# ConvNeXt-V2 block: smaller rstd batches, reordered GpSimd work, and one more slot between read and use

## Chip, cores, metric

The kernel runs on one core of a Trainium2 chip. The metric is device time in microseconds (us), the median of several executions.

## The reference, cut to what matters

```python
# x: 1 x 512 x 512 x 96 bf16; dw: 3x3 depthwise; w1: 96 -> 384; w2: 384 -> 96
out = depthwise_conv3x3(x, dw)
h = layernorm(out, axis=-1, eps=1e-5)
h = gelu_tanh(h @ w1)
gx = sqrt((h * h).sum(axis=(1, 2)) + 1e-6)          # over the whole image
nx = gx / (gx.mean(axis=-1) + 1e-6)
h = grn_gamma * (h * nx) + grn_beta + h
return x + h @ w2
```

The sum over the whole image cuts the kernel into two phases. Phase one computes convolution, layer norm, first matmul and GELU for all pixels and gathers statistics. Phase two, which needs these statistics, does the second matmul and writes the output. The change touches phase one only.

The layer norm divides by a standard deviation. Its reciprocal, called rstd, is computed for a batch of blocks at a time: six small operations on VectorE (DVE) give the variance and a first guess of the root, which Newton's iteration on GpSimd (POOL in the profiles) refines. PE and ACT are TensorE and ScalarE. `y_bf` is the convolution's output, `yn` the normalised block, `ynT` the same in the layout that the first matmul reads, and `gt` or `g` the output of GELU.

## The kernel before: the parts that matter

Phase one works in slots. A slot does the convolution of one block of 4 image rows (128 blocks) and, for an earlier block, each later stage. How many slots lie between the stages is set by constants, and each engine runs its own work in program order.

```python
NEWTON_ITERS = 3
LAG_ST, LAG_NORM, LAG_MLP = 2, 5, 3
# batches of blocks that share one rstd computation: 2, 2, 4, then 8 each
...
# conv_chunks(b), the end of a slot
act.activation(out=y[:], in_=Y[:], func=ACTF.Identity)              # y_bf <- Y, PSUM eviction
pool.tensor_tensor(out=q[:], in0=y[:], in1=y[:], op=ALU.mult)       # square: ysq <- y_bf
...
# stage_chain(k): six small DVE operations, mean, nmsq, var, clamp+eps, shift, seed of the root
# stage_newton(k): on GpSimd, 4 small operations in each Newton round
# stage_turn(k): DVE transpose rt <- rstd;  stage_rows(k): SP writes r_dram <- rt (4 DMAs)
# stage_bcast(k): SP reads rbc <- r_dram (4 DMAs)
# stage_norm(b):  GpSimd, yn <- y_bf * rbc
# stage_write(b): SP, yn_dram <- yn;   stage_read(b): SP, ynT <- yn_dram (changes the layout)
# mlp_units(b): per j: 4 matmuls U <- ynT,w1p, 2 GELUs gt <- U on ACT, 4 bn_stats on DVE;
#               for 3 blocks of 8 (RECOMP_PATTERN) SP also writes g_dram <- gt, 3 x 512 KB
...
put(last_s, ("chain", k))            # last_s: the slot of the batch's last statistics
put(last_s + 1, ("rows", k))
put(last_s + 3, ("bcast", k))
for b in batch:
    s = max(last_norm + 1, last_s + LAG_NORM)
    put(s, ("norm", b)); put(s + 1, ("write", b)); put(s + 2, ("read", b))
    put(s + LAG_MLP, ("mlp", b))
...
# the order of one slot in the program
write; load_x piece (transposing DMA xT <- x); read; bcast; load_x piece
norm
matmuls of MLP and convolution, interleaved; evac (with the square)
chain; newton; combine; turn; rows
```

A yn block is read in slot s+2 and used in slot s+3. All DMAs of the steady state are issued by SP (SyncE), one after the other; where one has to wait, the ones behind it wait too. In phase two, blocks of g that were stored are loaded, and the others are recomputed from yn.

## Time and profile before

| | before |
|---|---|
| median of 2 runs | 1887.39 us (1886.64 to 1888.15) |
| profiled span | 1883.5 us |
| phase one, to the end of the last bn_stats | 1296.2 us |
| the rest, phase two | 587.4 us |
| 8 slots, mean from the 32nd to the 112th y_bf eviction | (1022.7 - 271.0) / 10 = 75.2 us per 8 slots |

"32nd" counts from 0: the times at which ACT starts its y_bf evictions mark the slots.

The profile page of before: the span, the busy time of each engine, then DVE's busy share and PE's granted clock in 40 equal slices, in tenths.

```profile
span 1883.5 us, 58748 instructions
PE 1454.8 (77%) x25398; PEld 705.7 (37%) x25642; DVE 1443.5 (77%) x2340; ACT 1383.2 (73%) x1381; POOL 965.5 (51%) x733
...
DVE  2354586878878778778787788897788888888887
...
PEclk9887797888888878888888788696999999999999
```

No engine is full: DVE is mostly at 7 to 8 tenths in phase one (the first 27 slices), and PE's granted clock is mostly at 7 to 8 tenths where phase two has 9.

The table of windows of before, cut at the starts of eight successive y_bf evictions. Columns: busy us of each engine (number of instructions), granted clock, DMA share, GB/s. The share is the sum of packet times over 16 engines, so it can be above 1 where packets overlap. `...` stands for lines left out.

```profile
core 0: us, PE busy (x) PEld busy (x) DVE busy (x) ACT busy (x) POOL busy (x), PEclk, DMA share, GB/s
647.10:654.40 7.30, 6.69 (x144) 2.54 (x147) 7.17 (x13) 7.14 (x8) 5.82 (x3) 1.00 1.32 214
654.40:661.70 7.30, 5.25 (x117) 1.50 (x117) 7.13 (x17) 7.14 (x9) 4.73 (x7) 1.00 0.88 296
661.70:677.00 15.30, 11.25 (x168) 3.52 (x171) 9.95 (x18) 7.38 (x9) 13.33 (x14) 0.55 0.74 140
...
691.50:706.60 15.10, 9.45 (x144) 2.81 (x147) 8.23 (x14) 7.41 (x8) 5.86 (x3) 0.66 1.19 252
706.60:713.90 7.30, 6.32 (x142) 2.45 (x144) 6.45 (x11) 7.13 (x9) 5.77 (x2) 1.00 0.37 144
```

Six slots of eight take 7.3 us, in which ACT is full and DVE nearly so. Two take 15 us, with the clock down to 0.55 and 0.66; in and after them DMA runs partly empty (140 and 144 GB/s). The timelines show how a long slot begins. PE first, then SP for the time before it (start us, us, what, idle time before it and what ended it):

```profile
660.66 0.42 PE L37 MATMUL Y<-xT,Wd 32*32 32x511 bf16 x12
665.04 1.46 PE L37 MATMUL U<-ynT,w1p 128*128 128x512 bf16 x3 [3.95 <-DMA ynT<-yn_dram]
```

```profile
651.21 3.65 SPq L37 DMA_DIRECT2D g_dram<-gt  x3
654.96 0.55 SPq L37 DMA_DIRECT2D yn_dram<-yn  x1
655.60 1.59 SPq L37 DMA_TRANSPOSE xT<-in_x_dram  x1
657.25 0.57 SPq L37 DMA_DIRECT2D ynT<-yn_dram  x1
```

The read is issued at 657.25, behind three g writes, a yn write and a transpose. PE waits for it from 661.1, just before the next slot begins, and gets it at 665.0. The waits of before, first of engines, then of SP's own queue, from 300 to 1000 us (total us, times, longest):

```profile
DVE bst L37 <- ACT gt L37: 142.4, 73, 7.1
PE U L37 <- DMA ynT<-yn_dram: 125.6, 44, 7.6
```

```profile
SPq L37 <- ACT gt L37: 106.5, 54, 7.4
SPq L37 <- POOL yn L37: 50.7, 27, 2.4
SPq L37 <- DVE rt L37: 46.6, 9, 6.2
```

Besides g (`ACT gt`), SP waits for the normalise (`POOL yn`) before each write and, once per batch, for the transposed rstd (`DVE rt`) before the rows.

### The profile page before, as it was taken

How to read it: one execution, taken by the hardware profiler on the slowest of the kernel's cores; microseconds unless marked ns; L12 is line 12 of the kernel's file. 1: busy time of each engine (PE TensorE's matmuls, PEld its weight loads, DVE VectorE, ACT ScalarE, POOL GpSimd, SP SyncE). 2: the span in 40 equal slices, each digit the busy share in tenths (PEclk: the TensorE clock that was granted, in tenths of full speed). 3: DMA queues.
4: the chain of work that ended last, by engine and by line, in shares of the span. 5: the costliest groups of instructions: out<-in, count | busy, mean ns of one | idle time of the engine just before them, and what ended most of it. 6: DMA issues, size and time to landing. Idle time of an engine off the chain costs nothing.

```text
span 1883.5 us, 58748 instructions
## 1 busy us (share of the span) xinstructions
PE 1454.8 (77%) x25398; PEld 705.7 (37%) x25642; DVE 1443.5 (77%) x2340; ACT 1383.2 (73%) x1381; POOL 965.5 (51%) x733
## 2 busy tenths in 40 slices
PE   6778676777777777768777677462999999999998
PEld 3323222222222222222222222111666666666666
DVE  2354586878878778778787788897788888888887
ACT  2455586877878768778787688593887887887887
POOL 6765766768668667686686676621121121121120
PEclk9887797888888878888888788696999999999999
DMA  9996999899999998998999986564999999999996
GB/s 121 191 212 129 194 244 219 198 234 219 212 226 205 240 224 198 228 218 210 233 207 243 212 199 214 150 226 153 365 356 375 372 362 374 371 360 373 370 362 231
DMA packets 473012, 472.21 MB, mean 251 GB/s; under 512 B 298576, under 2 KB 394928, under 8 KB 472752
## 3 DMA queue, kind: packets, MB, share of 16 engines
q1 hardware_dynamic: 420144, 348.88, 73.0%
q0 software_dynamic: 20608, 88.09, 12.8%
q10 hardware_dynamic: 32000, 31.46, 5.5%
q8 instruction: 200, 3.28, 0.7%
q14 instruction: 60, 0.49, 0.1%
HBM read 224.55 MB, written 176.69 MB: 213 GB/s over the span
## 4 chain that ended last, share of the span: by engine, by line
PE 34%; ACT 18%; DMA 17%; DVE 5%; issue 4%; SPq 3%; another core or an unknown queue 2%; POOL 0%; ACTq 0%; DVEq 0%
DMA ynT<-yn_dram 16%; ACT gl L203 15%; PE U L37 10%; PE O L587 10%; PE Y L37 8%; DVE bst L37 5%; PE U L201 4%; SPq L37 3%; ACT y_bf L37 2%; PE S L37 2%; ACT gt L37 1%; DMA xr<-in_x_dram 0%; DMA out_dram<-o_sb 0%; DVE o_sb L589 0%
## 5 line engine op out<-in xcount | busy, mean ns | idle before, releaser
L37 DVE BATCH_NORM_STATS2 bst<-gt 128x6 f32<-128x512 bf16 x1536 | 928.3, 678 | 264.8 <-ACT gt L37 261.7
L37 ACT ACTIVATE gt<-U 128x1024 bf16<-128x1024 f32 x768 | 755.1, 1033 | 291.4 <-issue 185.1
L37 PE MATMUL U<-ynT,w1p 128*128 128x512 bf16 x1309 | 463.5, 436 | 267.9 <-DMA ynT<-yn_dram 213.2
L203 ACT ACTIVATE gl<-U 128x1024 bf16<-128x1024 f32 x480 | 457.6, 1028 | 106.2 <-PE U L201 98.1
L37 POOL TENSOR_TENSOR ysq<-y_bf 128x1536 bf16<-128x1536 bf16 x128 | 351.3, 2746 | 321.0 <-ACT y_bf L37 319.1
L37 PE MATMUL Y<-xT,Wd 32*32 32x512 bf16 x13806 | 414.9, 423 | 71.0 <-issue 21.3
L37 POOL TENSOR_TENSOR yn<-y_bf,rbc 128x1536 bf16<-128x1536 bf16 x128 | 395.0, 3089 | 6.7 <-DMA rbc<-r_dram 4.2
L587 PE MATMUL O<-W2s,gl 128*128 128x96 bf16 x6096 | 350.4, 206 | 19.7 <-ACT gl L203 5.1
L587 PEld LDWEIGHTS <-gl 128*128 128x128 bf16 x6096 | 304.2, 97 | 140.4 <-ACT gl L203 54.0
L37 PEld LDWEIGHTS <-w1p 128*128 128x128 bf16 x1536 | 115.1, 102 | 606.6 <-issue 343.0
L589 DVE TENSOR_TENSOR o_sb<-O,xb 128x384 bf16<-128x384 f32 x512 | 257.2, 551 | 100.0 <-PE O L587 90.1
L201 PE MATMUL U<-ynl,w1p 96*128 96x512 bf16 x960 | 283.4, 379 | 51.6 <-ACT gl L203 28.2
L187 POOL DMA_DIRECT2D xr<-in_x_dram x127 | 68.6, 540 | 433.8 <-DVE xb L578 376.6
L37 ACT ACTIVATE y_bf<-Y 128x1536 bf16<-128x1536 f32 x128 | 185.1, 1446 | 61.6 <-PE Y L37 61.6
L578 DVE TENSOR_TENSOR xb<-xr,B2bc_f 128x1536 f32<-128x1536 bf16 x127 | 222.8, 1755 | 9.1 <-DMA xr<-in_x_dram 6.3
L37 PEld LDWEIGHTS <-Wd 32*32 32x32 bf16 x13806 | 118.4, 89 | 272.5 <-issue 263.7
L201 PEld LDWEIGHTS <-w1p 96*128 96x128 bf16 x960 | 76.6, 98 | 88.5 <-issue 72.7
L37 PEld LDWEIGHTS <-y_bf 128*128 128x128 bf16 x1536 | 59.9, 101 | 36.1 <-issue 17.1
L37 PE MATMUL S<-rowsel,y_bf 128*128 128x4 bf16 x1536 | 59.1, 168 | 0.0
L37 PE MATMUL S<-rowsel,ysq 128*128 128x4 bf16 x1536 | 57.4, 167 | 0.0
L37 PEld LDWEIGHTS <-ysq 128*128 128x128 bf16 x1536 | 48.6, 99 | 0.0
L181 POOL DMA_DIRECT2D gl<-g_dram x71 | 37.6, 533 | 7.0 <-DVE W2s L552 3.9
(67 smaller groups left out, 224.9 us busy)
## 6 DMA issues: line engine op xcount, KB each, us to landing
g_dram<-gt SPq DMA_DIRECT2D x144, 512.0 KB, 5.9
yn_dram<-yn SPq DMA_DIRECT2D x128, 384.0 KB, 3.7
ynT<-yn_dram SPq DMA_DIRECT2D x128, 384.0 KB, 4.8
out_dram<-o_sb SPq DMA_DIRECT2D x128, 384.0 KB, 7.7
xr<-in_x_dram POOLq DMA_DIRECT2D x127, 384.0 KB, 7.4
gl<-g_dram POOLq DMA_DIRECT2D x71, 512.0 KB, 10.0
gl<-g_dram SPq DMA_DIRECT2D x70, 512.0 KB, 10.3
ynl<-yn_dram ACTq DMA_DIRECT2D x80, 384.0 KB, 11.5
```

The lines of the kernel that those rows point to most:

```text
L37: r = f(*a, **k)
L181: ld_engs[ldi[0] % 2].dma_start(out=gts[j][:], in_=g_dram[q, j])
L187: nc.gpsimd.dma_start(out=xr[:], in_=x[0, r0:r0 + GR].rearrange("r w c -> (r w) c").rearrange("(p g) c -> p g c", g=PXP))
L201: nc.tensor.matmul(U[:, i, :], lhsT=w1p[:C, j * 128:(j + 1) * 128], rhs=ynt[:, i0 + i, :], start=True, stop=True)
L203: nc.scalar.activation(out=perm_view(gts[j][:, :], i0, 2), in_=perm_src(U[:]), func=ACTF.Gelu_apprx_tanh)
L578: nc.vector.tensor_tensor(out=xb[:], in0=xr[:], in1=B2bc_f[:, None, :].to_broadcast([128, PXP, C]), op=ALU.add)
L587: nc.tensor.matmul(O[:, gl_, :], lhsT=gts[j][:, gg * 128:(gg + 1) * 128], rhs=W2s[:, j, :], start=(j == 0), stop=(j == NCH - 1))
L589: nc.vector.tensor_tensor(out=o_sb[:, sub * GPS:(sub + 1) * GPS, :], in0=O[:], in1=xb[:, sub * GPS:(sub + 1) * GPS, :], op=ALU.add)
```

## The change

Its intent: give GpSimd's normalise and square the right of way over Newton, let nothing on SP wait for the rstd, and leave the yn read another slot to land.

```diff
-NEWTON_ITERS = 3
+NEWTON_ITERS = 2
+BATCH = 4
-LAG_MLP = 3
+LAG_MLP = 4
@@ batches_of: 2, 2, 4, 8, 8, ... becomes 2, 2, 4, 4, ...; tiles and buffer counts follow
@@ the square leaves the eviction and is a stage of its own, a slot later
+        for b in range(NBLK):
+            put(b + 1, ("square", b))
             put(last_s, ("chain", k))
-            put(last_s + 1, ("rows", k))
+            put(last_s + 1, ("newton", k))
+            put(last_s + 1, ("turn", k))
+            put(last_s + 2, ("rows", k))
@@ the order of one slot
             for f in pieces:
                 f()
+            for k in get("rows"):
+                stage_rows(k)
             for b in get("norm"):
                 stage_norm(b)
+            for b in get("square"):
+                stage_square(b)
+            for k in get("newton"):
+                stage_newton(k)
+            for k in get("combine"):
+                combine(k)
@@ ... matmuls ...
+            for k in get("chain"):
+                stage_chain(k)
             if evac:
                 evac()
-            for k in get("chain"):
-                stage_chain(k)
-            for k in get("chain"):
-                stage_newton(k)
-            for k in get("combine"):
-                combine(k)
-            for k in get("rows"):
+            for k in get("turn"):
                 stage_turn(k)
-                stage_rows(k)
```

More of the change, by code (lines that the diff above doesn't have):

```diff
@@ L46, in batches_of @@
     out, b = [], 0
-    for n in (2, 2, 4):
-        if b + n <= nblk:
+    for n in (2, 2) + (BATCH,) * nblk:
+        n = min(n, nblk - b)
+        if n:
             out.append((b, n))
             b += n
-    while b < nblk:
-        n = min(8, nblk - b)
-        out.append((b, n))
-        b += n
     return out
@@ L84 @@
     NBLK = H // GR
+    NB = BATCH * GR * NG
     BATCHES = batches_of(NBLK)
@@ L213 @@
         xtpool = p1.enter_context(tc.tile_pool(name="xt", bufs=X_AHEAD + 3))
-        ypool = p1.enter_context(tc.tile_pool(name="ybf", bufs=8 + LAG_ST + LAG_NORM + 1))
+        ypool = p1.enter_context(tc.tile_pool(name="ybf", bufs=BATCH + 1 + LAG_ST + LAG_NORM + 1))
         ysqpool = p1.enter_context(tc.tile_pool(name="ysq", bufs=4))
         small = p1.enter_context(tc.tile_pool(name="small", bufs=2))
-        rtpool = p1.enter_context(tc.tile_pool(name="rt", bufs=2))
-        rbcpool = p1.enter_context(tc.tile_pool(name="rbc", bufs=3))
+        rtpool = p1.enter_context(tc.tile_pool(name="rt", bufs=3))
+        rbcpool = p1.enter_context(tc.tile_pool(name="rbc", bufs=4))
         ynpool = p1.enter_context(tc.tile_pool(name="yn", bufs=3))
@@ L288, in evac, with stage_square @@
                 ybf[b] = y
-                q = ysqpool.tile([128, NI, W], bf16, name="ysq")
-                pool.tensor_tensor(out=q[:], in0=y[:], in1=y[:], op=ALU.mult)
-                ysq[b] = q
             return [lambda n=n: tap(n) for n in range(9)], evac
+        def stage_square(b):
+            q = ysqpool.tile([128, NI, W], bf16, name="ysq")
+            pool.tensor_tensor(out=q[:], in0=ybf[b][:], in1=ybf[b][:], op=ALU.mult)
+            ysq[b] = q
         def stage_stats(b):
@@ L298, in stage_stats @@
             if b == b0:
-                Ss[k] = psS.tile([128, 2, 128], f32, name="S")
+                Ss[k] = psS.tile([128, 2, NB], f32, name="S")
             S = Ss[k]
@@ L313, in stage_chain @@
             S = Ss.pop(k)
-            mean = small.tile([128, 128], f32, name="mean")
+            mean = small.tile([128, NB], f32, name="mean")
             dve.tensor_scalar(out=mean[:, :N], in0=S[:, 0, :N], scalar1=1.0 / C, scalar2=None, op0=ALU.mult)
-            nmsq = small.tile([128, 128], f32, name="nmsq")
+            nmsq = small.tile([128, NB], f32, name="nmsq")
             dve.scalar_tensor_tensor(out=nmsq[:, :N], in0=S[:, 0, :N], scalar=-1.0 / C, in1=mean[:, :N],
                                      op0=ALU.mult, op1=ALU.mult)
-            var = small.tile([128, 128], f32, name="var")
+            var = small.tile([128, NB], f32, name="var")
             dve.scalar_tensor_tensor(out=var[:, :N], in0=S[:, 1, :N], scalar=1.0 / C, in1=nmsq[:, :N],
@@ L322, in stage_chain @@
             dve.tensor_scalar(out=var[:, :N], in0=var[:, :N], scalar1=0.0, scalar2=LN_EPS, op0=ALU.max, op1=ALU.add)
-            ri = small.tile([128, 128], i32, name="ri")
+            ri = small.tile([128, NB], i32, name="ri")
             dve.tensor_scalar(out=ri[:, :N], in0=var[:, :N].bitcast(i32), scalar1=1, scalar2=None,
@@ L336, in stage_newton @@
                 last = it == NEWTON_ITERS - 1
-                t_ = small.tile([128, 128], f32, name="nt")
+                t_ = small.tile([128, NB], f32, name="nt")
                 pool.tensor_tensor(out=t_[:, :N], in0=rcur, in1=rcur, op=ALU.mult)
@@ L340, in stage_newton @@
                 pool.tensor_scalar(out=t_[:, :N], in0=t_[:, :N], scalar1=-0.5, scalar2=1.5, op0=ALU.mult, op1=ALU.add)
-                rn = small.tile([128, 128], bf16 if last else f32, name="rstd" if last else "rn")
+                rn = small.tile([128, NB], bf16 if last else f32, name="rstd" if last else "rn")
                 pool.tensor_tensor(out=rn[:, :N], in0=rcur, in1=t_[:, :N], op=ALU.mult)
@@ L348, in stage_turn @@
             N = n * GR * NG
-            rt = rtpool.tile([128, 128], bf16, name="rt")
+            rt = rtpool.tile([128, NB], bf16, name="rt")
             dve.transpose(out=rt[:, :N], in_=rstds.pop(k)[:, :N])
@@ L365, in stage_bcast @@
             b0, n = BATCHES[k]
-            rbc = rbcpool.tile([128, 8, W], bf16, name="rbc")
+            rbc = rbcpool.tile([128, BATCH, W], bf16, name="rbc")
             for j in range(GR):
@@ L439 @@
         last_stat_slot = -1
+        for b in range(NBLK):
+            put(b + 1, ("square", b))
         for k, (b0, n) in enumerate(BATCHES):
             for b in range(b0, b0 + n):
-                s = b + LAG_ST
+                last_s = b + LAG_ST
                 if b == b0:
-                    s = max(s, last_stat_slot + 2)
-                put(max(s, b + LAG_ST), ("stats", b))
-                last_s = max(s, b + LAG_ST)
+                    last_s = max(last_s, last_stat_slot + 2)
+                put(last_s, ("stats", b))
             last_stat_slot = last_s
             put(last_s, ("chain", k))
-            put(last_s + 1, ("rows", k))
+            put(last_s + 1, ("newton", k))
+            put(last_s + 1, ("turn", k))
+            put(last_s + 2, ("rows", k))
             put(last_s + 3, ("bcast", k))
@@ L485 @@
             taps, evac = conv_chunks(s) if s < NBLK else ([], None)
-            for b in get("stats"):
-                pass
             stats = [lambda b=b: stage_stats(b) for b in get("stats")]
```

## The prediction

> **What bounds it now.** The table of windows puts phase two (1300 to 1883 us) at 355 GB/s and DMA share 1.00; the diff does not touch it. Phase one ends at about 1297 us (last bn_stats) and is not pinned to one engine: per 150 us between 300 and 1050, DVE is busy 119, ACT 115, PE 109 to 114, GpSimd 105. The starts of the y_bf evictions show why: per 8 blocks, six slots take 7.3 us and two about 15, 75 us in all. The 7.3 us slot is ACT's (1.45 + 6 x 1.03 us, slightly overlapped) and nearly DVE's (12 bn_stats, 7.21 us). In the long slots PE waits 4 to 6 us for ynT<-yn_dram (waits view: 129 us of these 750; 16% of the chain), then runs at a granted clock of 0.50 to 0.53 for about a slot. The Trainium skill, "TensorE: Matmul & The Clock Gate" (Part 1), has an idle PE at half clock; this trace agrees.
>
> The read is issued only a slot before use and lands in 4.1 to 9.3 us. Ahead of it in SyncE's order stand three 512 KB g_dram writes, transposes that back up (issue 1.2 to 5.2 us), or, once per batch, the rstd rows (SP waits 53 us in ten batches for rt) while GpSimd's Newton (5.6 us) and combine (1.7 us) delay the next normalise.
>
> **What the change does.** LAG_MLP 4 gives the read one more slot, 7.3 us or more: above the observed waits. Newton follows normalise and square and delays neither; normalise can run ahead. Newton: 12 operations of 0.30 to 0.45 us become 8 of 0.24 to 0.32, about 6 us per 8 blocks either way. Cost: DVE's chain and transpose run twice per 8 blocks, about 1.6 us each against 1.9 once: DVE needs 58 + 3.3 = 61.3 us per 8 blocks and becomes the engine floor. GpSimd needs 54.5. rbc and r_dram move the same bytes in twice the DMAs. Slots without MLP in between fall from six to two, the last MLP from slot 144 to 141.
>
> **Second limit: DMA.** Its share is 0.94, but some 16% of the time is nearly idle. I estimate DMA's demand at 58 to 63 us per 8 blocks, level with DVE, so I expect 65 to 67 us, not 58.
>
> **Sum.** Steady state: 12.5 groups of 8 x (75 - 66) = 113 us; ramp-up about 30; drain about 30. Total about 172 us, nearly all critical: the phases are serial.
>
> Predicted: 1715 us, range 1665 to 1790; faster by over 2%: 0.94, within 2%: 0.04, slower: 0.02.
>
> **Right if:** slots become even at 7.8 to 8.5 us; PE's wait for ynT falls from 213 us to under 60; phase one's granted clock rises from 0.85 towards 0.95; DVE is busy over 90% from 300 to 1050 us; GB/s there rises from 219 to about 250; phase two stays at 583 us.
>
> **Wrong if:** the transposes really need about 2 us of DMA each, as they took alone in the first 40 us (18 in 36): then DMA holds the slot near 8.8 us and the gain is about 80 us. The skill's "DMA: Bandwidth & Descriptors" (Issuing engines are not separate DMA queues) has all queues share 16 DMA engines; slack adds no bandwidth. Or if lagging DVE delays chain and transpose, and SP, waiting for rt, holds back g writes and reads, so that ynT waits return.

## The result, and the profile after

The changed kernel takes 1705.33 us (median of 2, 1702.93 to 1707.72), a ratio of 0.9035 with a 95% interval of 0.8979 to 0.9092.

| | before | after |
|---|---|---|
| start to 32nd eviction | 271.0 | 247.3 |
| 32nd to 112th eviction | 751.7 | 646.5 (64.6 per 8 slots) |
| 112th to last (127th) eviction | 138.5 | 115.8 |
| last eviction to end of last bn_stats | 135.0 | 109.8 |
| phase two | 587.4 | 581.7 |
| PE's wait for ynT, whole run | 213.2 | 66.0 |

Phase one gives 177 of the 182 us: 128 in the 95 slots after the 32nd, 24 at the start, 25 in the drain, where MLPs run with no convolution beside them. The same lines of the page as before:

```profile
span 1701.1 us, 59162 instructions
PE 1399.3 (82%) x25377; PEld 693.7 (41%) x25624; DVE 1476.4 (87%) x2445; ACT 1381.1 (81%) x1381; POOL 959.8 (56%) x781
...
DVE  2169999999999999999999999978888888888887
...
PEclk9899989989998999989999998869999999999999
```

DVE is now at nine tenths in nearly every slice of phase one, and phase one's granted clock at 8 or 9 tenths. The table of windows after, again cut at evictions (four of the eight slots that were looked at; the other four take 7.3 to 7.4 us), and below it how its long slot begins on PE:

```profile
core 0: us, PE busy (x) PEld busy (x) DVE busy (x) ACT busy (x) POOL busy (x), PEclk, DMA share, GB/s
642.90:650.20 7.30, 5.75 (x118) 1.71 (x120) 7.16 (x12) 7.14 (x8) 5.09 (x2) 1.00 1.41 228
650.20:657.50 7.30, 6.25 (x164) 2.67 (x165) 7.27 (x13) 7.13 (x8) 6.37 (x11) 1.00 0.98 293
657.50:670.20 12.70, 9.10 (x144) 2.59 (x147) 12.70 (x23) 7.40 (x8) 11.25 (x4) 0.73 1.14 253
670.20:677.50 7.30, 6.32 (x142) 2.46 (x144) 6.55 (x12) 7.13 (x9) 5.77 (x2) 1.00 1.10 314
```

```profile
660.33 1.04 PE L38 MATMUL U<-ynT,w1p 128*128 128x512 bf16 x4 [3.40 <-DMA ynT<-yn_dram]
```

One long slot is left in these eight. It too begins with PE waiting for ynT (3.40 us) and has a lowered clock (0.73). It differs from the first long one of before in two columns: DVE is busy for all of its 12.70 us, working off a backlog (23 operations in it, while ACT makes GELUs for about half as many), and DMA is not empty in it (253 GB/s). The waits after, from 300 to 1000 us, engines and then SP:

```profile
PE U L38 <- DMA ynT<-yn_dram: 44.0, 24, 5.5
DVE bst L38 <- ACT gt L38: 21.3, 25, 2.5
```

```profile
SPq L38 <- PE U L38: 99.7, 76, 3.7
SPq L38 <- PE Y L38: 24.1, 21, 2.5
SPq L38 <- ACT gt L38: 24.0, 39, 1.5
```

SP's waits for yn and rt have left the head of the list. It waits for PE to free buffers, so it runs ahead. PE still waits 44 us for ynT, but DVE only 21 us for GELUs, where it waited 142. The windows of the steady state say what has filled up instead, before and then after:

```profile
300.00:1000.00 700.00, 518.86 (x10560) 182.73 (x10706) 554.42 (x956) 535.92 (x521) 492.30 (x285) 0.86 0.95 221
```

```profile
300.00:1000.00 700.00, 575.80 (x12393) 207.80 (x12556) 674.45 (x1193) 625.67 (x612) 568.65 (x373) 0.94 1.15 255
```

DVE rises from 79% to 96% of the time, and DMA share from 0.95 to 1.15. Counted from the packet records in steps of 0.25 us over the same 700 us, DMA was less than half full in 15.3% of the steps before and in 0.8% after. So two resources look full after the change, and the profile alone doesn't say which one holds the time. It also doesn't say which part of the change did the work. The experiments ask both.

One more thing is new. DVE's timeline and GpSimd's, after:

```profile
647.05 0.23 DVE L38 SCALAR_TENSOR_TENSOR var<-S,nmsq 128x64 f32<-128x64 f32 x1
647.31 0.94 DVE L38 TENSOR_SCALAR var<-var 128x64 f32<-128x64 f32 x1
648.28 2.67 DVE L38 TENSOR_SCALAR ri<-var 128x64 int32<-128x64 int32 x1
```

```profile
645.11 3.09 POOL L38 TENSOR_TENSOR yn<-y_bf,rbc 128x1536 bf16<-128x1536 bf16 x1 [5.06 <-DMA rbc<-r_dram]
648.16 2.75 POOL L38 TENSOR_TENSOR ysq<-y_bf 128x1536 bf16<-128x1536 bf16 x1
```

Two tiny operations take 0.94 and 2.67 us, and each ends (648.25, 650.95) about 50 ns after a GpSimd operation ends (648.20, 650.91). Of the 99 such DVE operations 27 took over 0.4 us, and all 27 ended 37 to 56 ns after the end of a GpSimd operation; before it was 6 of 54. The Trainium skill, "SBUF — State Buffer" (Who interferes with whom), describes this: DVE and GpSimd share a port pair as an exclusive lock, which a `tensor_scalar` between SBUF tiles can need; the trace agrees. The operations that read PSUM (`var<-S,nmsq` and its like) stayed at 0.19 to 0.23 us. In the old order GpSimd had mostly just finished its square and waited for the chain. In the new order it is often in a square or a normalise. From 300 to 1000 us one batch's chain with its transpose sums to 2.7 us of DVE, where the prediction had 1.6.

### The profile page after: what moved, and what is told of

It is laid out like the page before. It is cut to its first block, busy times and chain, and to the rows that moved or that the text cites. A ratio compares the mean times of both kernels' runs of the same rounds, so it can differ in the third digit from the quotient of the medians.

```text
span 1701.1 us, 59162 instructions
## 1 busy us (share of the span) xinstructions
PE 1399.3 (82%) x25377; PEld 693.7 (41%) x25624; DVE 1476.4 (87%) x2445; ACT 1381.1 (81%) x1381; POOL 959.8 (56%) x781
## 5 line engine op out<-in xcount | busy, mean ns | idle before, releaser
L38 PE MATMUL U<-ynT,w1p 128*128 128x512 bf16 x1303 | 433.9, 407 | 134.2 <-ACT gt L38 66.8
L38 PE MATMUL Y<-xT,Wd 32*32 32x512 bf16 x13806 | 394.4, 401 | 72.9 <-ACT y_bf L38 28.2
L38 PEld LDWEIGHTS <-w1p 128*128 128x128 bf16 x1536 | 110.7, 99 | 444.0 <-issue 339.5
L38 PEld LDWEIGHTS <-y_bf 128*128 128x128 bf16 x1536 | 56.2, 97 | 26.2 <-issue 5.9
L38 DVE TENSOR_SCALAR mean<-S 128x64 f32<-128x64 f32 (+1 forms) x33 | 6.8, 207 | 49.3 <-PE S L38 49.3
```

Source lines behind the costliest of these rows:

```text
L38: r = f(*a, **k)
```

## The experiments

"Per 8" is the time from the 32nd to the 112th eviction over 10, and "phase one" the end of the last bn_stats, both of the profiled run. Each experiment ran in 3 rounds (e1 to e4, e5 to e8 and e9 to e12 together); the kernel before had medians of 1885.63 to 1888.21 us beside them. The kernel after ran in rounds of its own, so that it meets the experiments only by its ratio. All outputs are right.

| run | median us | ratio (95%) | per 8 | phase one |
|---|---|---|---|---|
| before | 1887.39 | | 75.2 | 1296 |
| after | 1705.33 | 0.9035 (0.8979 to 0.9092) | 64.6 | 1119 |
| e1 before, LAG_MLP 4 | 1725.09 | 0.9154 (0.9123 to 0.9186) | 64.4 | 1132 |
| e2 after, LAG_MLP 3 | 1760.80 | 0.9360 (0.9318 to 0.9402) | 68.4 | 1174 |
| e3 after, batches of 8 | 1710.39 | 0.9080 (0.9050 to 0.9109) | 63.8 | 1126 |
| e4 after, chain's tail on GpSimd | 1703.49 | 0.9033 (0.9003 to 0.9063) | 64.4 | 1118 |
| e5 after, 2 of 8 stored | 1722.81 | 0.9127 (0.9113 to 0.9140) | 60.7 | 1068 |
| e6 e4 and e5 together | 1718.87 | 0.9110 (0.9096 to 0.9123) | 60.4 | 1063 |
| e7 before, new order only | 1771.29 | 0.9402 (0.9372 to 0.9431) | 67.6 | 1178 |
| e8 before, batches of 4 only | 1890.49 | 1.0025 (1.0006 to 1.0044) | 76.9 | 1299 |
| e9 after, old order | 1695.43 | 0.8994 (0.8962 to 0.9025) | 64.4 | 1112 |
| e10 after, 3 Newton rounds | 1700.67 | 0.9029 (0.8979 to 0.9079) | 64.0 | 1115 |
| e11 after, stores moved to the drain | 1673.05 | 0.8866 (0.8825 to 0.8907) | 61.9 | 1080 |
| e12 e11 and e4 together | 1671.80 | 0.8862 (0.8823 to 0.8901) | 62.4 | 1092 |

### e1: the slack alone

```diff
 # on before
-LAG_MLP = 3
+LAG_MLP = 4
```

> The kernel before with LAG_MLP 4 alone (batches of 8, three Newton rounds, old order). Theory A, late yn reads: the one slot of slack between read and use is most of the gain; about 1745 us (1715 to 1780), PE's wait for ynT from 300 to 1050 us falls from 129 us to under 50. Rival B, GpSimd order and batch size: slack alone gives little; 1840 us or more, ynT waits over 90 us.

Measured: 1725 us, inside theory A's range. One constant gives 161 us of the 182, and the steady state is that of the full change (64.4 per 8). The wait for ynT is down from 125.6 us:

```profile
PE U L37 <- DMA ynT<-yn_dram: 33.5, 23, 3.2
```

What the full change has over it, some 20 us, lies outside the steady state, and is a difference of two effects. e1 needs 136 us from its last eviction to its last bn_stats (995.5 to 1132.0), where the changed kernel needs 110, as its last MLP comes in slot 145, not in slot 141, and its phase two is 6 us longer (587.5 us). But it reaches its 32nd eviction 15 us earlier (232.4 us, where the changed kernel has 247.3).

### e2: the change without the slack

```diff
 # on after
-LAG_MLP = 4
+LAG_MLP = 3
```

> The changed kernel with LAG_MLP back at 3. Theory A, late yn reads: most of the gain is lost, about 1830 us (1790 to 1870), two long slots per 8 come back. Rival B, GpSimd order and batch size: it stays near 1740 us or below.

Measured: 1761 us, below the range of theory A and above that of theory B: both missed. Without slack the rest of the change still gains 126 us. So the two halves of the change are substitutes for the most part: 161 and 126 do not add up to 182.

### e7 and e8: which part of the rest

e7 is before with the new order on GpSimd and SP (square, Newton, turn and rows as in the change), with batches of 8, LAG_MLP 3 and three Newton rounds; rbc has 3 and rt 2 buffers as before, y_bf one more than before (17). e8 is before with batches of 4 only:

```diff
 # e8, on before
-        n = min(8, nblk - b)
+        n = min(4, nblk - b)
```

> Old slack and batches of 8, three Newton rounds; only the new order is kept (square a slot later after normalise, Newton after both, rstd rows a slot later). The changed kernel with LAG_MLP 3 gained 126 us; this and the next run say from which part. Theory A2, order: normalise runs ahead, so writes and reads leave earlier: 1740 to 1800 us. Rival B2, batches of 4: 1850 to 1890.

> The kernel before with batches of 4 alone. Theory A2, order: Newton now delays normalise twice per 8 blocks and SP waits for rt twice, so 1860 to 1920 us, apart from some 20 us won at the start by fewer bubbles. Rival B2, batches of 4: 1780 or less.

Measured: 1771 us and 1890 us, both inside the ranges of theory A2. The order alone gains 117 us; smaller batches alone gain nothing. The side remark on e8, some 20 us won at the start, was wrong: its 32nd eviction comes at 286.1 us, 15 later than in before, and only its drain is shorter (107.9 instead of 135.0 us). SP's waits, 300 to 1000 us, show the mechanism. First e7, then e8:

```profile
SPq L38 <- ACT gt L38: 158.9, 88, 5.9
...
SPq L38 <- DVE rt L38: 8.8, 9, 1.6
SPq L38 <- POOL nt L38: 5.1, 8, 1.3
SPq L38 <- POOL rn L38: 1.1, 1, 1.1
```

```profile
SPq L37 <- DVE rt L37: 133.8, 19, 10.4
```

A wait is put down to the GpSimd operation that came last, so yn's waits in e7 are the POOL lines together (a third one, of 0.2 us, is left out). With the new order they are 6 us where before had over 50, and those for rt are 8.8 instead of 46.6: in e7 the median normalise is over 5.8 us before its write is issued, in before 0.5 us. SP's waits fall less as a whole, from 305 to 251 us: it now comes early at the g writes (158.9 us, where before had 106.5). PE's wait for ynT in the same 700 us falls from 125.6 to 64.0 us, so the order cures about half of it. With twice as many batches in the old order, the wait for rt grows to 133.8 us, and everything behind it in SP's order waits too. In the changed kernel the new order takes this cost away, or the slack hides it (e9).

### e9: the slack and the batches of 4, old order

```diff
 # on after: square in the slot of its eviction, Newton in the slot of its chain, both after evac
-            put(b + 1, ("square", b))
+            put(b, ("square", b))
-            put(last_s + 1, ("newton", k))
+            put(last_s, ("newton", k))
```

> The changed kernel (batches of 4, LAG_MLP 4, two Newton rounds) with the old order on GpSimd: square right after the eviction, Newton right after the chain and ahead of the next normalise. If the slack alone brings phase one to DMA's limit (the other lag-4 kernels all ran about 64.5 us per 8 blocks), the order is worth nothing on top: 1695 to 1725 us. If Newton ahead of normalise still costs with batches of 4 (alone they gained nothing): 1740 or more.

Measured: 1695 us, if anything faster than the changed kernel, though the intervals overlap. Once the read has its extra slot, the order of GpSimd's work is worth nothing with batches of 4. The rows are still issued a slot later here, so this run doesn't try that part of the change by itself.

### e3 and e10: batch size and Newton rounds on top of the rest

e3 is the changed kernel with batches 2, 2, 4, 8, 8, ... (one rbc and one rt buffer fewer, so that it fits). e10 has `NEWTON_ITERS = 3`.

> The changed kernel with batches of 8 again (2, 2, 4, then 8; one rbc and one rt buffer fewer so that it fits). Theory A, late yn reads: batch size is not what matters, 1685 to 1735 us: DVE saves one chain per 8 blocks (about 2.7 us measured with its waits), some 30 us lost again to bubbles at the start and a longer drain. Rival B, batch size: 1780 us or more.

> The changed kernel with three Newton rounds: 1.4 us more on GpSimd per batch of 4, about 57 of 64.5 us per 8 blocks. Theory: GpSimd is not the limit, 1697 to 1715 us. If it is: 1720 or more.

Measured: 1710 and 1701 us, both as the theory said and neither distinct from the changed kernel. Of the 30 us that batches of 8 were expected to lose at both ends, e3 lost 10: its drain is 26 us longer (135.4 us), but its 32nd eviction comes 15 us earlier (231.8 us). e3 is also e1 with the new order, the later rows, two Newton rounds and one more y_bf buffer, and in the same rounds it is 15 us faster, with intervals that don't meet. So with batches of 8 these together are still worth a little beside the slack; which of them, no run says. GpSimd, at 81% of the steady state after the change (568.65 of 700 us), is not its limit.

### e4, e5, e6: what limits phase one now

e4 takes the port waits away from DVE:

```diff
 # on after, stage_chain loses its last three operations; stage_newton begins with
+            pool.tensor_scalar(out=var[:, :N], in0=var[:, :N], scalar1=0.0, scalar2=LN_EPS, op0=ALU.max, op1=ALU.add)
+            pool.tensor_scalar(out=ri[:, :N], in0=var[:, :N].bitcast(i32), scalar1=-0.5, scalar2=float(0x5F3759DF),
+                               op0=ALU.mult, op1=ALU.add)
```

e5 takes g writes away from phase one; e6 is both.

```diff
 # e5, on after
-    RECOMP_PATTERN = [False, True, True, False, True, True, False, True]
+    RECOMP_PATTERN = [False, True, True, True, False, True, True, True]
```

> The changed kernel with the last three operations of DVE's chain, the fp32 and int32 SBUF to SBUF tensor_scalar ones, done as two operations on GpSimd. In the profile after, 21 of these from 150 us on took 0.5 to 2.7 us instead of 0.2, each ending about 50 ns after a GpSimd operation. Theory C, DVE is the limit now and loses about 1.0 us per batch to the wait for GpSimd's port: DVE needs 59.7 instead of 63.3 us per 8 blocks, total falls by 35 to 55 us to about 1660. Rival D, DMA is the limit now (share 1.11, nearly never idle): total stays within 12 us of 1705.

> The changed kernel with 2 of 8 blocks of g stored instead of 3 (the recompute pattern), so that phase one writes about 1.6 MB of 16 MB less per 8 blocks; the result stays right, phase two recomputes 16 blocks more. Theory D, DMA is phase one's limit after the change: phase one's end falls from 1118 us, but only to DVE's own 63.3 us per 8 blocks (chain with its port waits): to 1095 to 1108. Rival C, DVE alone is the limit: stays within 5 us of 1118. Phase two 585 to 610 us either way; the total is not the test.

> The same with the chain's last three operations on GpSimd as well. If DMA and DVE are near-equal limits after the change (each removed alone shows little), removing both shows: phase one's end falls to 1060 to 1085 us, about 61 us per 8 blocks, total 1650 to 1685. If neither is the limit: end of phase one over 1100.

Measured, e4: 1703 us, so theory D. DVE's busy time in the 700 us fell from 674 to 643 us and the slots did not move. The port waits cost DVE time that it had. e1 and e9 say the same: they run at 64.4 us per 8 with DVE busy for 647 and 657 us. Measured, e5: phase one ends at 1068, even below theory D's range. The windows of e5 from 300 to 1000 us:

```profile
300.00:1000.00 700.00, 614.18 (x12714) 215.99 (x12713) 692.77 (x1272) 660.82 (x651) 599.08 (x401) 0.97 1.12 241
```

With a tenth of the traffic gone, slots go from 64.6 to 60.7 us per 8, DVE is at 99%, and PE's wait for ynT is 5 us. So the DMA path was the limit of the changed kernel, through reads that came late (PE waited 44 us for ynT there), and DVE is the next. DMA's share is still 1.12 in e5: a high share by itself does not say that DMA is the limit. 96 bn_stats of 0.60 us and two chains of 1.7 us are 61 us per 8 blocks. My range for e5 was off because I had counted DVE's floor with the port waits (2.7 us per chain). In e5 they mostly don't occur: 11 of 99 operations took over 0.4 us, and the chain is back at 1.7 us. Why they vanish there was not tried. They are as few with the old order (e9: 10 of 99, 1.6 us per chain) and with the new order and batches of 8 (e3: 5 of 54), so the new order does not bring them by itself. e6 gains only 5 us more in phase one; by then ACT, at 7.3 us per slot or 58.2 per 8, is near (60.4 measured), but that it is the limit there was not shown. The totals of e5 and e6 are worse than the changed kernel's, because phase two grew from 582 to 654 us; I had expected 585 to 610, and so a total for e6 that it missed.

### e11 and e12: using it

In the drain, after the last convolution, DMA is not full: from 1010 to 1070 us of the changed kernel its share is 0.67. So e11 stores as many blocks of g as before (48), but the last 14 all belong to them, and only 34 of the first 114. Phase two takes the blocks in an order that keeps its mix of loaded and recomputed ones.

```diff
 # on after
-    def is_recomp(q):
-        return RECOMP_PATTERN[q % len(RECOMP_PATTERN)]
+    TAIL, EARLY = 14, 34
+    HEAD = NBLK - TAIL
+    stored = [b for b in range(HEAD) if b * EARLY // HEAD != (b - 1) * EARLY // HEAD] + list(range(HEAD, NBLK))
+    redone = [b for b in range(NBLK) if b not in stored]
+    s_, r_ = iter(stored), iter(redone)
+    ORDER = [next(s_) if i % 8 in (0, 3, 6) else next(r_) for i in range(NBLK)]
+
+    def is_recomp(q):
+        return q not in stored
 # and phase two walks through ORDER instead of range(NBLK)
```

> The changed kernel with the same 48 stored blocks of g, but 14 of them the last 14 (in the drain, where DMA is at half load) and 34 spread over the other 114; phase two takes the blocks in an order that keeps its old mix. DMA as phase one's limit says 2.4 instead of 3 stored blocks per 8 take about 62 us: phase one ends at 1085 to 1100, phase two stays at 583 to 595, total 1675 to 1695. If DMA is not the limit: 1700 or more.

> The same with the chain's last three operations on GpSimd, so that DVE needs about 59.5 instead of 61 to 63 us per 8 blocks: phase one ends at 1070 to 1095, total 1660 to 1690, at most 15 us below the run before.

Measured: 1673 and 1672 us, 11% better than before in the same rounds; against the changed kernel, which ran in other rounds, the medians are 2% lower. e9 and e10, which equal the changed kernel within the noise, ran in e11's rounds and took 1695 and 1701 us. e11 did slightly better than its ranges: phase one ends at 1080 us (1085 to 1100 expected). In e11 the steady state takes 61.9 us per 8, and phase two stays at 582 us. Adding e4's edit is again worth nothing that can be told from noise: single runs of either kernel spread from 1664 to 1679 us.

## Why the prediction was right

- **Total.** 1715 us was predicted, 1705 measured. The terms: steady state 113 against 128 us measured, start 30 against 24, drain 30 against 25, and 6 us that were not predicted between the phases and in phase two.
- **Start and drain, in part luck.** The only reasons that the prediction names for these two terms come from the smaller batches: fewer slots without MLP and an earlier last one. Batches of 4 alone (e8) gain 12 us in the two together, as they lose 15 at the start; the slack alone (e1) gains 37, all of it at the start. The sum of 49 us comes mainly from the slack.
- **Cause.** Late ynT reads: right. Slack alone (e1) brings the steady state to where the full change has it. The half clock came and went with these waits (0.86 before, 0.94 in e1); no run changed it alone. The prediction names the new order too, but did not see that it is a second cure for the same wait, which gives 117 us by itself (e7): once normalise runs ahead, writes and reads leave SP earlier. With the slack and batches of 4 in place it brings nothing (e9).
- **"Slots become even at 7.8 to 8.5 us":** right in the mean (8.1), wrong in form. Most slots keep ACT's 7.3 us, and in each eight one or two take 8 to 15.
- **Second limit.** DMA's demand was estimated at 58 to 63 us per 8 blocks, "level with DVE", and 65 to 67 us expected. Measured: 64.6, with the DMA path the limit (e5) and DVE's floor just below. The DVE term was mis-sized, 3.3 us for two chains and transposes against 5.4 measured, as it left out the port waits; e4 shows that this did not matter.
- **Signs.** PE's wait for ynT fell to 66 us (predicted: under 60, so just missed), the clock from 300 to 1000 us rose from 0.86 to 0.94 (towards 0.95), DVE is at 96% (over 90%), DMA at 255 GB/s (about 250). Phase two takes 582 us; it was to stay as it was, and by the same cut it took 587 before.
- **Feared, not seen.** The transposes did not hold the slot at 8.8 us. SP was not held by rt.

What stays open: e5 took away g writes, and with them both bytes for the 16 DMA engines and issues on SP's queue. The Trainium skill, "Perfetto Trace Analysis" (What "DMA-bound" means), tells these two apart, the DMA engines and the issuing sequencer. The packet records, with engines less than half full in only 0.8% of the steps, speak for the engines; no run moved issues to another queue to show it. No run gave the read still more slack either: as the changed kernel still waits for ynT, a part of what is left may be reads that land late in a burst and not the DMA engines' throughput. What the later rstd rows are worth by themselves was not tried either.

## What to carry to other kernels

When an in-order consumer waits for a DMA that shares its queue with bursts, look first at how many slots lie between issue and use. One constant gave nearly nine tenths of this gain, and it costs a buffer's lifetime, not work (the ring of four ynT buffers was there before). Parts of a change that cure the same wait do not add up, so try each alone and each left out before calling one of them the cause. When the wait is gone, ask what is full next and where that resource is empty: here the stores moved into the drain, where DMA had room, brought another 2%.

## What the Trainium skill lacked or had wrong

- "TensorE: Matmul & The Clock Gate" (Part 1) gives about 3.4 us of sustained work to bring the full clock back. In the long slot of before shown above, PE worked again from 665.04 us, busy for 10.8 of 11.6 us with two gaps of 0.36 us, and the windows have it at 0.50 until 676.6 us:

```profile
665.00:668.40 3.40, 3.36 (x64) 2.14 (x76) 1.97 (x5) 1.94 (x2) 3.32 (x5) 0.50 0.15 29
...
675.20:676.60 1.40, 1.40 (x15) 0.21 (x14) 0.47 (x1) 0.54 (x1) 0.48 (x1) 0.50 0.98 165
676.60:680.00 3.40, 2.81 (x65) 1.52 (x78) 2.47 (x4) 3.40 (x4) 1.50 (x1) 1.00 0.94 258
```

- "SBUF — State Buffer" gives about 115 ns for a GpSimd DMA descriptor to follow the DVE operation that held the shared port pair (A bandwidth-pool intuition that's wrong). For a DVE operation held up by a GpSimd one it has a ratio, "DVE 6.8× slower", but no time from the end of the one to the end of the other. Here, in the kernel after, operations of 0.2 us grew to as much as 3.0 us, and all 27 long ones ended 37 to 56 ns after a GpSimd operation. Nor does it say that one DVE operation can be passed over more than once: in e5 one took 6.9 us, across the end of a square, a normalise and another square.
